# Scaled eviction of the dK, dV accumulator: from ScalarE to VectorE

## The chip, the cores and the metric

The kernel runs on one core of a Trainium2 chip. The metric is the device time of one execution in microseconds (us). The engines are TensorE (PE in the profile; PEld is its weight load), VectorE (DVE), ScalarE (ACT), GpSimd (POOL) and SyncE (SP, which here issues DMAs).

## The reference

The program computes a transformer block (adaptive layer norm, attention with 32 heads of 16 columns, layer norm, a squared-ReLU MLP) on 2048 tokens of width 512, and the gradients of its inputs by jax.vjp. What matters here is attention:

```
qkv = (x @ wqkv).reshape(B, S, 3, H, Dh).transpose(2, 0, 3, 1, 4)
q, k, v = (qkv[0], qkv[1], qkv[2])
scale = Dh ** (-0.5)
scores = jnp.einsum('bhqd,bhkd->bhqk', q, k) * scale
p = _softmax(scores, axis=-1)
o = jnp.einsum('bhqk,bhkd->bhqd', p, v)
```

Its backward pass needs, per head, P again from q and k, dP = dO V^T, dS = P * (dP - rowsum(dO * O)), dV = P^T dO, dK = scale * dS^T Q and dQ = scale * dS K. (The kernel folds the row sum and the softmax's denominator into operands, so that dS is one multiplication of the PSUM result dP by the exponentials.)

## The kernel before

The program runs in phases: projections and the forward attention, with the MLP and its gradients worked in between (0 to about 1170 us of the profile), the backward attention loop (`attn_bwd`, about 1170 to 2420 us), and the remaining weight gradients and the gradient of x. The change touches the loop alone.

The loop goes over 8 groups `g` of four heads, two pairs `jp` in each, four **chunks** `c` of 512 keys, and 16 blocks `ib` of 128 queries, in groups of `G = 4` blocks; `i` is the block's place in its group. So there are 8 x 2 x 4 = 64 chunks of 16 blocks. One block, called a step below, does for each of two heads `a`:

- TensorE: scores into `st` (L1568, three PSUM buffers), and, one block behind, dP into `dp` (L1494, three PSUM buffers);
- ScalarE: the exponential of `st` into `pu` (L1571);
- VectorE: dS = `dp` * `pu` into the bf16 tile `ds` (L1498).

In every second group of four blocks (`off`, L1500) the multiplication of the first block's second head goes another way: ScalarE copies `dp` to SBUF (L1506) and GpSimd multiplies (L1507). In the other groups TensorE transposes a part of `ds` itself (`turn_ds`, L1527) and ScalarE copies it to `dsT` (L1528). The rest of `ds` is transposed by a DMA that SyncE issues (L1515).

Some blocks later, every second block calls `kv_two`, which calls `kv` (L1442) for two blocks: eight matmuls add dS^T Q and P^T dO into `acckv`, one PSUM tile of 128x512 (L1448). The blocks between call `dq` (L1470), which adds dS K into `accq`. `acckv` has a single buffer. After the 16th block of a chunk, `kv` moves it to the bf16 tile `kvT`, scaled per partition by `kvs` (L1451): `kvs` holds 0.25 on the first 64 partitions (dK) and 1 on the others (dV). The matmuls run four or five blocks behind, so this eviction comes in the fourth step (`i` = 3) of the first group of the next chunk, behind that step's scores, exponentials and dS. The next chunk's first accumulator matmul must wait for it. When the four chunks of a pair of heads are done, `turn` transposes `kvT` back on TensorE (L1459) and ScalarE copies it out (L1463); `accq` is scaled by the constant 0.25 on VectorE (L1477).

Order: in this phase the instructions of TensorE, SyncE and GpSimd run in the order in which the program writes them. Those of VectorE and ScalarE are ordered by the scheduler that builds the program. Each engine runs its own instructions in order.

Of the kernel before, what the change touches and what calls it, by code (L numbers as in the profile page):

```python
# [11 lines left out]
ACT = mybir.ActivationFunctionType  # L12
ALU = mybir.AluOpType
# [92 lines left out]
class K:  # L106
# [1315 lines left out]
    def attn_bwd(self):  # L1422
# [7 lines left out]
        tc, nc = self.tc, self.nc  # L1430
# [5 lines left out]
        acckv = accp.tile([P, 512], F32, name="acckv")  # L1436
        nc.vector.memset(acckv[:], 0.0)
        accq = accp.tile([P, ST, 2, DH], F32, name="accq")
        masked, kvs = self.masked, self.kvs
        pend, pendq = [], []  # L1440

        def kv(u):  # L1442
            (T, g, jp, c, ib, kvT, pu, ds) = u
            for j, (n, src) in enumerate((("Q", ds), ("dO", pu))):
                for a in range(2):
                    r = 64 * j + 32 * a
                    col = (2 * jp + a) * DH
                    nc.tensor.matmul(acckv[r:r + DH, :], lhsT=T[n][:, ib, col:col + DH], rhs=src[:, a, :],  # L1448
                                     start=(ib == 0), stop=(ib == ST - 1))
            if ib == ST - 1:  # L1450
                nc.scalar.activation(kvT[:, 512 * c:512 * (c + 1)], acckv[:], ACT.Copy, scale=kvs[:])  # L1451

        def turn(g, jp, kvT, s0):

# [24 lines left out]
        def kv_two(n=2):  # L1479
            for u in pend[2 - n:2]:  # L1480
                kv(u)
            (T, g, jp, c, ib, kvT, pu, ds) = pend[1]
            del pend[:2]
            if c % 2 and ib == ST - 1 and (g, jp) == (NQ - 1, 1):
                turnq.append((g, jp, kvT, 4 * (c - 1)))
            elif c == SC - 1 and ib == ST - 1:
                turnq.extend((g, jp, kvT, s0) for s0 in (0, ST // 2))
# [45 lines left out]
        for g in range(NQ):  # L1533
            for jp in range(2):
# [13 lines left out]
                kvT = kvp.tile([P, S], BF16, name="kvT")  # L1548
# [36 lines left out]
        with tc.manual_schedule(engines=ALL):  # L1585
            for t in (2, 0):
                for p in self.wq_pieces(t):
                    nc.gpsimd.dma_start(*p)
            for a in range(2):
                dP(last, a)  # L1590
            dS(last)
            while len(pend) > 2:
                kv_two()
            kv(pend[0])
            for _ in range(G):
                dq(pendq.pop(0), [0, 1])
            kv_two(1)
            k0, v0, k1 = [dpp.tile([P, 512], F32, name="dp") for _ in range(3)]
            self.dw_mm(k0, 1, 0, 0, ST // 2)
            turn(*turnq.pop(0))  # L1600
            for _ in range(G):
                dq(pendq.pop(0), [0, 1])
            self.dw_mm(v0, 2, 0, 0, ST // 2)
            self.dw_mm(k0, 1, 0, ST // 2, ST)
            self.col_sum(1)
            self.dw_mm(v0, 2, 0, ST // 2, ST)
            self.col_sum(2)
            self.cs_bc(1)
            while pendq:
                dq(pendq.pop(0), [0, 1])  # L1610
            self.cs_bc(2)
            self.dw_mm(k1, 1, 1, 0, ST)
# [312 lines left out]
```

## Time and profile before

| | |
|---|---|
| median of 3 runs | 2545.73 us (2542.11 to 2547.05) |
| the profiled execution | 2545.66 us, of which the span is 2543.9 |
| busy over the span | PE 2453.8, ACT 2299.9, DVE 1700.3, POOL 707.1 us |
| DVE L1498, dS | 1920 of 681 ns, busy 1169.9 us |
| ACT L1571, exponentials | 2048 of 626 ns, busy 1075.8 us |
| ACT L1451, the eviction | 64 of 687 to 717 ns, first start 1194.4, last 2418.0 us |
| PE L1448, accumulator matmuls | 4096 |

A group's row gives the line, the engine, the operation, what is written and read, the number, then busy time and mean ns of one, and the idle time of the engine just before it with what ended it. In a view in order of time the columns are start, length, engine, line and operation, with neighbours of one kind merged into one row (x13); the idle time before the first of them stands in brackets. PE's ends are modelled, so its matmuls overlap in the rows and its busy share reads high. Two instructions of one engine can overlap by their pipelining: busy time of a row is then less than number times mean.

### The profile page before, as it was taken

To read this page: it belongs to the slowest core of one execution; us is meant where nothing else is said; L and a number is where in the kernel's file an instruction comes from. 1 tells how busy PE (TensorE), PEld (TensorE's weight loads), DVE (VectorE), ACT (ScalarE), POOL (GpSimd) and SP (SyncE) were. 2 spreads that over 40 slices of the span, in tenths; PEclk is the share of its full clock that TensorE was granted. 3 is DMA by queue.
4 is the path that set the end of the run, shared out by engine and by line. 5 is a ranking of instruction groups with operands and counts; after the bars stand their busy time and mean duration, and the time that the engine had idled before them with its cause. 6 is when DMAs were issued, how large, how long until landed. Compare 5 with 4: busy or idle time off the path is not lost.

```text
span 2543.9 us, 76653 instructions
## 1 busy us (share of the span) xinstructions
PE 2453.8 (96%) x30727; PEld 1201.3 (47%) x30727; DVE 1700.3 (67%) x3523; ACT 2299.9 (90%) x3757; POOL 707.1 (28%) x1265
## 2 busy tenths in 40 slices
PE   8999899999999999999999999999999999999998
PEld 4555555555555554663444444444444444443443
DVE  6222223423332343677999999999999999999957
ACT  7999999999999997436999999999999999999935
POOL 2454521220231031354222222222222222222223
PEclk9999999999999999999999999999999999999999
DMA  4588652440351053898999999999999999999996
GB/s 165 117 179 197 169 106 80 103 116 23 107 135 49 22 162 102 165 208 197 221 219 216 217 217 218 218 216 213 216 219 217 219 218 214 217 220 233 231 211 175
DMA packets 1258571, 442.07 MB, mean 174 GB/s; under 512 B 1203540, under 2 KB 1227222, under 8 KB 1258214
## 3 DMA queue, kind: packets, MB, share of 16 engines
q1 hardware_dynamic: 1219078, 336.03, 68.1%
q0 software_dynamic: 37056, 100.11, 13.2%
q8 instruction: 240, 3.93, 0.6%
q10 hardware_dynamic: 2080, 1.05, 0.1%
q14 instruction: 117, 0.96, 0.1%
HBM read 73.73 MB, written 62.40 MB: 54 GB/s over the span
## 4 chain that ended last, share of the span: by engine, by line
PE 58%; ACT 26%; DMA 8%; issue 5%; DVE 2%; POOL 1%; SPq 0%; DVEq 0%; ACTq 0%; POOLq 0%
ACT pu L391 18%; PE st L1568 15%; PE st L388 8%; PE acckv L1448 8%; PE accq L1470 7%; DMA dsT<-ds 7%; ACT pu L1571 6%; PE accbank L322 3%; PE dp L1494 2%; PE dps L1047 2%; PE pps L1234 2%; PE dp L1618 1%; PE pps L631 1%; PE dps L992 1%; PE st L1713 1%
## 5 line engine op out<-in xcount | busy, mean ns | idle before, releaser
L1498 DVE TENSOR_TENSOR ds<-dp,pu 128x512 bf16<-128x512 f32 x1920 | 1169.9, 681 | 67.9 <-PE dp L1494 46.6
L1571 ACT ACTIVATE pu<-st 128x512 bf16<-128x512 f32 x2048 | 1075.8, 626 | 49.1 <-PE st L1568 21.3
L391 ACT ACTIVATE pu<-st 128x1024 bf16<-128x1024 f32 x992 | 912.0, 1077 | 3.1 <-PE st L388 2.9
L388 PE MATMUL st<-QTm,KTq 128*128 128x512 bf16 x1984 | 587.7, 377 | 19.5 <-ACT pu L391 6.0
L322 PEld LDWEIGHTS <-pu 128*128 128x128 bf16 x8192 | 347.6, 96 | 235.7 <-issue 2.3
L322 PE MATMUL accbank<-Vaug,pu 128*128 128x17 bf16 x8192 | 357.7, 171 | 1.2 <-ACT Vaug L522 0.9
L1470 PEld LDWEIGHTS <-dsT 128*128 128x128 bf16 x8192 | 240.1, 96 | 229.4 <-issue 199.8
L1494 PE MATMUL dp<-m,q 64*128 64x512 bf16 x1024 | 344.4, 382 | 1.6 <-DVE g2w L1053 0.7
L1494 PE MATMUL dp<-m,dOTg 64*128 64x512 bf16 x1024 | 344.2, 382 | 0.1
L1568 PE MATMUL st<-m,QTg 64*128 64x512 bf16 x1024 | 322.1, 381 | 12.2 <-ACT pu L1571 7.5
L1568 PE MATMUL st<-m,q 64*128 64x512 bf16 x1024 | 321.6, 382 | 11.3 <-ACT pu L1571 6.7
L388 PEld LDWEIGHTS <-KTq 128*128 128x128 bf16 x1984 | 187.9, 96 | 176.1 <-issue 124.5
L1507 POOL TENSOR_TENSOR ds<-junk,pu 128x512 bf16<-128x512 f32 x64 | 74.1, 1157 | 412.6 <-ACT junk L1506 412.6
L302 POOL DMA_DIRECT2D QTm<-QTq_d x124 | 63.1, 511 | 341.0 <-PE st L388 319.5
L1448 PE MATMUL acckv<-ds,Qg 128*16 128x512 bf16 x1024 | 154.5, 382 | 0.0
L1448 PE MATMUL acckv<-pu,dOg 128*16 128x512 bf16 x1024 | 154.4, 382 | 0.0
L1448 PE MATMUL acckv<-pu,q 128*16 128x512 bf16 x1024 | 154.0, 381 | 0.0
L1448 PE MATMUL acckv<-ds,q 128*16 128x512 bf16 x1024 | 154.0, 381 | 0.0
L1470 PE MATMUL accq<-Kg,dsT 128*128 128x16 bf16 x4096 | 143.7, 170 | 10.3 <-DMA dsT<-ds 9.9
L1507 POOL TENSOR_TENSOR ds<-csq,pu 128x512 bf16<-128x512 f32 x64 | 73.9, 1154 | 281.5 <-ACT csq L1506 281.5
L1470 PE MATMUL accq<-q,dsT 128*128 128x16 bf16 x4096 | 144.6, 170 | 3.8 <-DMA dsT<-ds 3.6
L329 DVE RECIPROCAL rl<-accbank 128x4 f32<-128x4 f32 x128 | 22.9, 179 | 159.6 <-PE accbank L322 159.4
(383 smaller groups left out, 2980.3 us busy)
## 6 DMA issues: line engine op xcount, KB each, us to landing
KTq<-KTq_d POOLq DMA_DIRECT2D x24, 512.0 KB, 4.0
duT_d<-auT POOLq DMA_DIRECT2D x3, 1792.0 KB, 7.9
aT_d<-rT POOLq DMA_DIRECT2D x3, 1792.0 KB, 11.3
KTq_d<-KTq SPq DMA_DIRECT2D x32, 128.0 KB, 1.8
QTq_d<-ev_fm SPq DMA_DIRECT2D x32, 128.0 KB, 3.9
VTq_d<-vT POOLq DMA_DIRECT2D x4, 1024.0 KB, 6.5
dsT<-ds SPq DMA_TRANSPOSE x256, 7.2
dx<-dx_d SPq DMA_DIRECT2D x16, 256.0 KB, 5.6
```

The source lines that it names most:

```text
L302: nc.gpsimd.dma_start(QTm[j][32 * j:32 * j + 32, :], self.QTq_d[g, 32 * j:32 * j + 32, 512 * qc:512 * (qc + 1)])
L322: nc.tensor.matmul(acc[:, a, sub, :], lhsT=pu[:, a, sub * P:(sub + 1) * P], rhs=Vaug[:, kb, h, :], start=(kb == 0 and a == 0 and sub == 0) ...
L388: nc.tensor.matmul(stt[:, a, :], lhsT=KT[:, kb * P:(kb + 1) * P], rhs=QTm[2 * jp + a][:], start=True, stop=True)
L391: nc.scalar.activation(pu[:], stt[:], ACT.Exp, scale=self.scale)
L1047: nc.tensor.matmul(pt[:], lhsT=a[st], rhs=g_tm[:, st, :], start=(st == 0), stop=(st == ST - 1))
L1448: nc.tensor.matmul(acckv[r:r + DH, :], lhsT=T[n][:, ib, col:col + DH], rhs=src[:, a, :], start=(ib == 0), stop=(ib == ST - 1))
L1470: nc.tensor.matmul(accq[:, ib, a, :], lhsT=dsT[:, (i * 2 + a) * 4 + sub, :], rhs=T["K"][:, 4 * c + sub, col:col + DH], start=(c == 0 and i ...
L1494: nc.tensor.matmul(dp[:], lhsT=T["dOT"][rd, ib * P:(ib + 1) * P], rhs=masked["VT"][2 * jp + a][rd, 512 * c:512 * (c + 1)], start=True, sto ...
L1498: nc.vector.tensor_tensor(dsg[:, i, a], dp[:], pu[:, a, :], ALU.mult)
L1507: nc.gpsimd.tensor_tensor(dsg[:, i, 1], f[:], pu[:, 1, :], ALU.mult)
L1568: nc.tensor.matmul(stt[:], lhsT=T["QT"][rs, q], rhs=masked["KT"][2 * jp + a][rs, c0:c0 + 512], start=True, stop=True)
L1571: nc.scalar.activation(pu[:, a, :], stt[:], ACT.Exp, scale=self.scale)
```

## The change

The eviction is computed by VectorE's `tensor_scalar` with the per-partition scalar `kvs`, in place of ScalarE's activation with the same scalar as its scale. Input, output, formats and place in the program are as before.

```diff
             if ib == ST - 1:
-                nc.scalar.activation(kvT[:, 512 * c:512 * (c + 1)], acckv[:], ACT.Copy, scale=kvs[:])
+                nc.vector.tensor_scalar(kvT[:, 512 * c:512 * (c + 1)], acckv[:], kvs[:], None, ALU.mult)
```

## The prediction

> **What bounds the kernel now.** I began with the share of busy time by stage, because the line that changes runs only in the backward attention loop (1172 to 2418 us). Two of its 64 chunks, and 200 us of it, look like this (columns: length, then busy time and instructions of PE, its weight loads, DVE, ACT, POOL, then clock, DMA share, GB/s):
>
> ```profile
> core 0: us, PE busy (x) PEld busy (x) DVE busy (x) ACT busy (x) POOL busy (x), PEclk, DMA share, GB/s
> 1600.00:1800.00 200.00, 195.12 (x2756) 82.28 (x2752) 188.82 (x311) 194.72 (x391) 46.21 (x90) 1.00 1.13 217
> ```
>
> ACT is busy 97%, DVE 94%, PE 98% (with modelled ends). By these shares VectorE has the room. A share says nothing about where in a chunk it lies, so I read the order of time next: first VectorE alone, then ScalarE, then TensorE, around the eviction of one chunk.
>
> ```profile
> 1811.57 7.85 DVE L1498 TENSOR_TENSOR ds<-dp,pu 128x512 bf16<-128x512 f32 x13
> 1819.91 3.74 DVE L1498 TENSOR_TENSOR ds<-dp,pu 128x512 bf16<-128x512 f32 x6 [0.49 <-PE dp L1494]
> 1823.90 5.47 DVE L1498 TENSOR_TENSOR ds<-dp,pu 128x512 bf16<-128x512 f32 x9 [0.25 <-PE dp L1494]
> ```
>
> Thirteen multiplications of 0.68 us take 7.85: one starts every (7.85 - 0.68) / 12 = 0.598 us, which is also the median of all 1920. VectorE has no hole in the stretch in which the eviction runs; its hole (0.49 in this view) comes behind it, where GpSimd takes one multiplication.
>
> ```profile
> 1816.31 1.09 ACT L1571 ACTIVATE pu<-st 128x512 bf16<-128x512 f32 x2
> 1817.28 0.70 ACT L1451 ACTIVATE kvT<-acckv,kvs 128x512 bf16<-128x512 f32 x1
> 1817.85 2.09 ACT L1571 ACTIVATE pu<-st 128x512 bf16<-128x512 f32 x4
> 1819.76 0.66 ACT L1506 COPY junk<-dp 128x512 f32<-128x512 f32 x1
> ```
>
> ```profile
> 1816.81 0.39 PE L1568 MATMUL st<-m,q 64*128 64x512 bf16 x1
> 1817.90 0.39 PE L1494 MATMUL dp<-m,q 64*128 64x512 bf16 x1
> 1818.52 0.37 PE L1568 MATMUL st<-m,q 64*128 64x512 bf16 x1 [0.23 <-ACT pu L1571]
> 1818.53 0.39 PE L1494 MATMUL dp<-m,q 64*128 64x512 bf16 x1
> 1818.84 0.39 PE L1448 MATMUL acckv<-ds,q 128*16 128x512 bf16 x2
> 1819.38 0.39 PE L1494 MATMUL dp<-m,q 64*128 64x512 bf16 x1
> ```
>
> Elsewhere a step's first exponential starts 0.42 to 0.47 us after its score matmul starts (medians at 9 of a chunk's 16 steps; the matmul's own 0.37 is in it), so there ScalarE has no queue. Behind the eviction it has one: the scores of 1816.81 are read only at 1817.85, and TensorE stands at 1818.52 for a score buffer.
>
> For VectorE I went by single records. There are three dP buffers, so a dP matmul needs the multiplication three before it to have ended. It starts 0.05 us after that end, held by VectorE, at 10 of the 32 places of a chunk (medians over 62 chunks), three in each group but the one behind the eviction: in three of four groups VectorE paces TensorE and not the reverse. The commonest period of a chunk is 18.89 us. VectorE's 30 multiplications take 30 x 0.598 = 17.94 of it; 0.95 is idle, nearly all in the two holes: 0.57 (median) in the group behind the eviction, 0.31 in the other group that gives one to GpSimd. The two holes have the same program around them, except that the first has the eviction ahead of it on ScalarE. I read their difference, 0.26, as ScalarE's lag.
>
> **The change part by part.** *Removed:* 64 ScalarE instructions of 0.70 us. The exponential behind one starts 0.57 after it, so ScalarE is relieved by 64 x 0.57 = 36 us. That shortens the loop only where ScalarE's lag reaches VectorE: 0.26 per chunk.
>
> *Added:* 64 VectorE instructions. Their shape, 128x512 f32 in PSUM to bf16, has two near rows:
>
> ```profile
> L1212 DVE TENSOR_SCALAR rT<-pps,bias 128x512 bf16<-128x512 f32 x42 | 31.5, 751 | 105.4 <-PE pps L1209 105.4
> L1477 DVE TENSOR_SCALAR dq_t<-accq 128x512 bf16<-128x512 f32 x16 | 10.9, 681 | 18.0 <-PE accq L1470 18.0
> ```
>
> L1477 scales by a constant: 0.681, and the next instruction starts 0.598 after it. L1212 takes its scalar per partition from SBUF, as the new instruction does (kvs): 0.751, and 0.667 at its shortest to the next start. Scalar_tensor_tensor shows the same split, 691 with constants and 750 with a per-partition operand, so the 0.07 belongs to the operand and not to L1212's second operation. I take 0.67; bounds 0.60 and 0.75 (no overlap with the next).
>
> [...]
>
> *Where it lands.* In program order the eviction follows the two multiplications of step 4 of a chunk's first group. In the stretch shown these are the 9th and 10th of the thirteen (starts 1816.35 and 1816.95), so it starts at 1817.55. Its last accumulator matmuls start at 1816.49 and last 0.38, so it waits for nothing (0.68 to spare). Queued behind it are the 11th to 13th; TensorE waits for them through the dP buffers. Then:
> - The 11th starts at 1818.22 instead of 1817.55 and ends at 1818.90.
> - The second dP matmul of step 6, which needs that buffer, starts at 1818.95 instead of 1818.53: +0.42. Its loss of 0.67 is cut by 0.25 because the old start stood behind ScalarE (1818.52 above).
> - The accumulator matmuls follow 0.31 later, the next dP 0.54 after those, at 1819.80; VectorE starts 0.53 after it, at 1820.33 instead of 1819.91. It was free at 1820.01: the hole is now 0.32, as in the other group.
> - From there TensorE catches up, since ScalarE no longer holds it at step 8, but VectorE runs without a break and takes back only the 0.04 to 0.05 of idle time there.
>
> So each chunk grows by 0.37 to 0.42; I take 0.39. The sum by slots agrees: 17.94 + 0.67 + 2 x 0.31 + 0.07 = 19.30 against 18.89, +0.41. The next chunk's first accumulator matmul must now wait for VectorE rather than ScalarE; it stands behind the dP matmul that already waits for the 11th multiplication, so that wait costs nothing more. No DMA is issued by the moved step. The turns of kvT come three steps behind and move with TensorE; in the 16 chunks that have them TensorE's transposes follow the same dP matmul, so they shift by the same amount. Of the 64 evictions the last lies in the tail, where both engines wait for TensorE (2.2 us): 0.05 there at most.
>
> *Against it:* TensorE's waits for the transposed dS, which lands 7.2 us after its issue (median), sum to 23.6 us on its weight loads. Transfers issued ahead of the eviction and read behind it gain its delay. VectorE's idle time at those two places is 3.4 and 1.8 us over the loop (means over medians); I let 4 us of it go.
>
> Sum: 63 x 0.39 = 24.6, less 4, about **+20 us**. The profiled execution took 2545.66 us, of which 2543.9 are its span and 1.8 lie around it; the median of the runs is 2545.73, so it serves as the base: 2545.7 + 20 = **2566 us**. By the bounds of the price (0.60 and 0.75, gaining 0.32 and 0.47 per chunk, all 5 or none absorbed): 2561 and 2575.
>
> **The rivals.** *The holes take it in (2546 us).* VectorE's order is not written by hand in this phase (only TensorE's, SyncE's and GpSimd's are), so the eviction could be placed behind the 13th multiplication, in the hole. Then 0.57 of its 0.67 is covered and the rest, 0.10 x 63 = 6 us, goes against the ScalarE lag and the waits for dS. For it: 0.95 idle per chunk exceeds 0.67. Against it: it is ready 0.68 before the 11th, so nothing calls for a later place.
>
> *ScalarE is the pace (2532 us).* Its 97% and the chain of waits, where exponentials have more of the loop than VectorE, speak for it. If its load causes both holes, a chunk falls to 17.94 + 0.67 + 0.07 = 18.68, -0.21 x 63 = -13 us. It decides if TensorE is still found waiting for exponentials where VectorE is free. Against it: exponentials mostly start as soon as their scores are there, and TensorE waits for a score buffer only 14.0 us in the whole loop.
>
> *Nothing comes back from ScalarE (2588 us).* If the hole of 0.57 has another cause, such as the copy for GpSimd (0.66 here, 0.59 in the other group), the whole price stays: 63 x 0.67 = 42 us.
>
> **How the numbers follow.** Chances: forecast 0.66, holes take it in 0.12, ScalarE the pace 0.09, nothing back 0.13. A change within 0.2% (5 us, 2541 to 2551) can't be told from none here. The forecast's own range is 2556 to 2576; to hold 8 in 10 it reaches down into the second case and up to the last, 2549 to 2588. Faster 0.09, same 0.12, slower 0.66 + 0.13 = 0.79.
>
> **What would show it.** VectorE's row for L1451: 64 of about 0.75 us, no idle time before them; 0.68 or 0.70 would mean the per-partition operand is free. The commonest chunk about 19.3 us. The waits of L1568 for exponentials (14.0 us) nearly gone, ScalarE about 94% busy and VectorE 97%. The hole behind the eviction at 0.3. I am wrong if the eviction stands in that hole, if chunks without a turn stay at 18.89, or if the hole stays at 0.57.

## The result and the profile after

| | before | changed |
|---|---|---|
| median of 6 runs each, side by side | 2541.42 us | 2563.23 us (2559.0 to 2566.08) |
| ratio | | 1.0083, 95% interval 1.0067 to 1.0100 |
| span of the profiled execution | 2543.9 us | 2563.8 us |
| commonest chunk / mean chunk of the loop | 18.89 / 19.47 us | 19.23 / 19.78 us |

The kernel is 22 us slower (17 to 25 by the interval). The spans differ by 19.9; the mean chunk grew by 0.306, and 63 x 0.306 = 19.3: in these two executions the loss lies in the loop.

Two rows of the groups of the changed kernel, and its 200 us of the loop by stage (columns as before):

```profile
L1498 DVE TENSOR_TENSOR ds<-dp,pu 128x512 bf16<-128x512 f32 x1920 | 1171.4, 680 | 49.2 <-PE dp L1494 45.2 <-ACT pu L1571 1.6 <-ACT junk L1506 0.2
L1451 DVE TENSOR_SCALAR kvT<-acckv,kvs 128x512 bf16<-128x512 f32 x64 | 47.3, 739 | 0.7 <-PE acckv L1448 0.7
```

```profile
core 0: us, PE busy (x) PEld busy (x) DVE busy (x) ACT busy (x) POOL busy (x), PEclk, DMA share, GB/s
1600.00:1800.00 200.00, 195.10 (x2738) 78.05 (x2731) 193.46 (x320) 190.50 (x377) 46.90 (x92) 1.00 1.10 214
```

The eviction takes 0.739 us and waits for nothing but 0.7 us once, in the tail. ScalarE fell from 97% to 95% busy, VectorE rose from 94% to 97%. The same chunk as before, first VectorE, then ScalarE, then TensorE, in order of time:

```profile
1823.81 6.06 DVE L1498 TENSOR_TENSOR ds<-dp,pu 128x512 bf16<-128x512 f32 x10
1829.79 0.74 DVE L1451 TENSOR_SCALAR kvT<-acckv,kvs 128x512 bf16<-128x512 f32 x1
1830.45 1.87 DVE L1498 TENSOR_TENSOR ds<-dp,pu 128x512 bf16<-128x512 f32 x3
1832.55 9.06 DVE L1498 TENSOR_TENSOR ds<-dp,pu 128x512 bf16<-128x512 f32 x15 [0.23 <-PE dp L1494]
```

```profile
1828.56 3.07 ACT L1571 ACTIVATE pu<-st 128x512 bf16<-128x512 f32 x6
1831.59 0.58 ACT L1506 COPY junk<-dp 128x512 f32<-128x512 f32 x1
```

```profile
1830.35 0.38 PE L1568 MATMUL st<-m,q 64*128 64x512 bf16 x1
1831.18 0.37 PE L1494 MATMUL dp<-m,q 64*128 64x512 bf16 x1 [0.46 <-DVE ds L1498]
1831.48 0.39 PE L1448 MATMUL acckv<-ds,q 128*16 128x512 bf16 x2
1832.03 0.39 PE L1494 MATMUL dp<-m,q 64*128 64x512 bf16 x1
```

VectorE evicts without a hole on either side (1829.79, next start 1830.45: a slot of 0.66). The multiplication behind it ends at 1831.13 (1830.45 + 0.68), and TensorE's second dP matmul of step 6 starts at 1831.18. Before, the score matmul beside it stood for ScalarE; now it goes at 1830.35 and the dP matmul stands for VectorE. Over the loop (1200 to 2400 us; waits: us in total, times, longest) the one wait has taken the other's place, and that for the transposed dS has not shrunk:

```profile
PE st L1568 <- ACT pu L1571: 13.7, 55, 0.3
PEld L1470 <- DMA dsT<-ds: 23.6, 43, 1.8
```

```profile
PEld L1470 <- DMA dsT<-ds: 26.3, 41, 1.9
PE dp L1494 <- DVE ds L1498: 24.9, 57, 0.5
```

The first two lines are of before, the others of the changed kernel, which has no wait of `st` for `pu` among its waits. The hole behind the eviction (extra time between two multiplications, median over 62 chunks) fell from 0.57 to 0.31.

### The profile page after: what moved, and what is told of

The parts are those of the page before. It is cut to its first block, busy times and chain, and to the rows that moved or that the text cites. A ratio compares the mean times of both kernels' runs of the same rounds, so it can differ in the third digit from the quotient of the medians.

```text
span 2563.8 us, 76589 instructions
## 1 busy us (share of the span) xinstructions
PE 2469.2 (96%) x30727; PEld 1182.4 (46%) x30727; DVE 1737.7 (68%) x3587; ACT 2285.6 (89%) x3693; POOL 706.8 (28%) x1265
## 4 chain that ended last, share of the span: by engine, by line
PE 63%; ACT 19%; DMA 8%; DVE 4%; issue 4%; POOL 1%; DVEq 0%; SPq 0%; ACTq 0%; POOLq 0%
ACT pu L391 18%; PE st L1568 17%; PE acckv L1448 9%; PE st L388 8%; PE accq L1470 8%; DMA dsT<-ds 7%; PE dp L1494 4%; PE accbank L322 3%; DVE ds L1498 2%; PE dps L1047 2%; PE pps L1234 2%; PE dp L1618 1%; PE pps L631 1%; DVE kvT L1451 1%; PE st L1713 1%
## 5 line engine op out<-in xcount | busy, mean ns | idle before, releaser
L1568 PE MATMUL st<-m,q 64*128 64x512 bf16 x1024 | 312.4, 381 | 1.0
L1568 PE MATMUL st<-m,QTg 64*128 64x512 bf16 x1024 | 312.4, 381 | 0.9
```

The source lines that it names most:

```text
L1568: nc.tensor.matmul(stt[:], lhsT=T["QT"][rs, q], rhs=masked["KT"][2 * jp + a][rs, c0:c0 + 512], start=True, stop=True)
```

## The experiments

Chunk times and holes below come from the single records of each trace, as medians over chunks 2 to 63. A chunk is counted "with turns" when `turn` runs in it, which is every fourth. The times were taken in three sets, each beside its own runs of before (medians 2547.74, 2543.88 and 2546.70 us): the first four kernels below in one, the next three and the one in the hole in another, the rest in the last. Means and waits come from the one profiled execution of each kernel. In the code, `...` marks lines left out.

**No eviction at all.** `kvT` is one tile, zeroed once:

```diff
-                nc.scalar.activation(kvT[:, 512 * c:512 * (c + 1)], acckv[:], ACT.Copy, scale=kvs[:])
+                pass
...
-                kvT = kvp.tile([P, S], BF16, name="kvT")
+                kvT = kvT0
```

> Leaves out: the eviction of the accumulator altogether (dK and dV come from a zeroed tile). All else is the kernel before. Theory (VectorE paces; ScalarE's eviction costs only the lag that reaches VectorE behind it): the hole behind the old place of the eviction shrinks from 0.57 to 0.31 us, the commonest chunk from 18.89 to 18.63, the time by 63 x 0.26 = 16 us. Rival 1 (the longer hole has another cause, such as the copy for GpSimd): no change. Rival 2 (ScalarE is the pace): 0.57 per chunk, 36 us faster.

Measured: 2532.59 us, ratio 0.9943 (0.9925 to 0.9960), that is 10 to 19 us faster; commonest chunk 18.58; hole 0.31. The hole of 0.57 was ScalarE's lag: the copy for GpSimd is still there and the hole is not. What ScalarE's eviction cost the loop was 0.31 per chunk, and relieving ScalarE of its 0.57 was worth no more than that. The time is as forecast. The mean chunk fell only from 19.47 to 19.32 in the profiled execution, which was the slowest of the five (2543.45 us, 11 over their median); in it TensorE's waits for the transposed dS grew:

```profile
PEld L1470 <- DMA dsT<-ds: 43.9, 62, 3.7
```

**The eviction split between the engines by partitions.**

```diff
-                nc.scalar.activation(kvT[:, 512 * c:512 * (c + 1)], acckv[:], ACT.Copy, scale=kvs[:])
+                sl = slice(512 * c, 512 * (c + 1))
+                nc.scalar.activation(kvT[0:64, sl], acckv[0:64], ACT.Copy, scale=kvs[0:64])
+                nc.vector.tensor_scalar(kvT[64:P, sl], acckv[64:P], kvs[64:P], None, ALU.mult)
```

> The eviction split by partitions: ScalarE moves 0 to 63, VectorE 64 to 127, so each engine pays a whole instruction (its length goes by the 512 columns). Theory (TensorE's second dP matmul of step 6 waits for the later of the two engines, so the two delays do not add): as the changed kernel, commonest chunk 19.23, about 21 us slower than before (within 4). Rival (the price and ScalarE's lag add up): 63 x 0.66 = 42 us slower than before, chunk 19.55.

Measured: 2578.30 us, ratio 1.0124 (1.0105 to 1.0143): 31 us slower, chunk 19.47, between the two. It doesn't decide. Each part did cost a whole instruction or nearly: 0.757 us on VectorE and 0.677 on ScalarE for 64x512, against 0.739 and 0.702 for 128x512. VectorE's part was placed one multiplication later than in the changed kernel, and its slot is longer (first VectorE's rows, then ScalarE's):

```profile
1501.41 3.07 DVE L1498 TENSOR_TENSOR ds<-dp,pu 128x512 bf16<-128x512 f32 x5
1504.52 0.76 DVE L1451 TENSOR_SCALAR kvT<-acckv,kvs 64x512 bf16<-64x512 f32 x1
1505.31 1.29 DVE L1498 TENSOR_TENSOR ds<-dp,pu 128x512 bf16<-128x512 f32 x2
```

```profile
1503.54 0.68 ACT L1451 ACTIVATE kvT<-acckv,kvs 64x512 bf16<-64x512 f32 x1
1504.11 2.04 ACT L1571 ACTIVATE pu<-st 128x512 bf16<-128x512 f32 x4
```

ScalarE's part had ended 0.30 us before VectorE's started (1503.54 + 0.68 = 1504.22). But VectorE's starts 0.04 after the multiplication ahead of it has ended (1504.48), and the next multiplication 0.03 after its own end (1505.28), where in the changed kernel it overlaps both by 0.08. So its slot, counted as the extra time between the two multiplications around it, is 0.90 instead of 0.66. Why the overlap is lost was not tested.

**The hole moved ahead of the eviction, the eviction on ScalarE.** In the kernel before:

```diff
-            return (c * SC + ib // G) % 2 == 1
+            return (c * SC + ib // G) % 2 == 0
```

> The kernel before (eviction on ScalarE) with the parity of off() turned over: GpSimd takes its multiplication in groups 1 and 3 of a chunk counted from 1, the group of the eviction among them, and not in the one behind it. Theory: ScalarE's lag behind the eviction now meets a group in which VectorE has a queue of dP in hand, so it no longer opens a hole: chunk 18.63, 16 us faster than before. Rival (the lag costs its 0.26 wherever it falls): no change. Rival (moving the copy for GpSimd beside the eviction makes ScalarE later still): slower by some us.

Measured: 2544.74 us, ratio 0.9990 (0.9970 to 1.0011): no difference that can be told. The commonest chunk did fall to 18.58, both holes at 0.31, a little below the 18.63 expected; the time did not follow. The chunks with turns grew from 20.54 to 20.85, and the waits for the transposed dS doubled (in an execution of 2554.12 us, the slowest of ten):

```profile
PEld L1470 <- DMA dsT<-ds: 52.1, 81, 2.5
```

**The same turn of parity with the eviction on VectorE.**

> The changed kernel (eviction on VectorE) with the parity of off() turned over as in the run before. Theory: VectorE's work is 30 x 0.598 + 0.66 and two holes of 0.31 per chunk wherever the holes lie, so chunk 19.23 and the time of the changed kernel, about 21 us slower than before (within 4). Rival (a hole in the same group lends its idle time to the eviction): 0.31 per chunk back, about 2 us slower than before.

Measured: 2578.77 us, ratio 1.0126 (1.0106 to 1.0145): 31 us slower. The chunk is 19.24 and both holes 0.31, as the theory has it: a hole earlier in the same group lends the eviction nothing. The time is some 10 us over what was expected: the chunks with turns are longer again (21.16 against 20.86, some 5 us in all), and the waits for dS are about twice those of the changed kernel (51.7 against 26.3 us).

**The changed kernel again**, as the base for the next two and for the one in the hole.

> The changed kernel again, beside the next runs on one chip: about 21 us slower than before.

Measured: 2570.99 us, ratio 1.0104 (1.0087 to 1.0120); chunk 19.23. That is 27 us over before (22 to 31), where the runs side by side above had 22 (17 to 25): with the same commonest chunk, the cost in time came out 5 us apart.

**A constant in place of the per-partition operand.**

```diff
-                nc.vector.tensor_scalar(kvT[:, 512 * c:512 * (c + 1)], acckv[:], kvs[:], None, ALU.mult)
+                nc.vector.tensor_scalar(kvT[:, 512 * c:512 * (c + 1)], acckv[:], 1.0, None, ALU.mult)
...
-                nc.scalar.copy(d, v[:, t, :, :, 0:DH])
+                nc.scalar.activation(d, v[:, t, :, :, 0:DH], ACT.Copy, scale=1.0 if t else self.scale)
```

> The changed kernel with the constant 1.0 as VectorE's scalar; the factor 0.25 of dK is applied by ScalarE's copies out of the turned tile, which are instructions of the kernel already. Theory (the per-partition operand makes the eviction's slot 0.66 instead of 0.60): eviction 0.68 long, chunk 19.16 to 19.17, 4 us faster than the changed kernel. Rival (the slot is set by the shape alone): no difference.

Measured: 2566.35 us, ratio to before 1.0090 (1.0072 to 1.0107), 4.6 us below the base by the medians. The intervals overlap, so the time does not settle it. The trace settles the slot: the row of the eviction has 678 ns where the changed kernel has 739, its slot is 0.60 and the commonest chunk 19.17. The mean chunk did not fall with it (19.81 in the profiled execution of either), so a gain in time is not shown.

```profile
L1451 DVE TENSOR_SCALAR kvT<-acckv 128x512 bf16<-128x512 f32 x64 | 43.4, 678 | 0.7 <-PE acckv L1448 0.7
```

**The eviction twice on VectorE** (the changed line written twice).

> The changed kernel with the eviction done twice on VectorE, same input and output. Theory (nothing is left to regain from ScalarE and VectorE has no usable room): the second one costs its whole slot, 0.66 x 63 = 42 us more than the changed kernel, chunk 19.89. Rival (VectorE's two holes of 0.31 take in a part): about 20 us more.

Measured: 2596.41 us, ratio 1.0214 (1.0194 to 1.0235): 25 us over the base, chunk 19.57, which is 0.34 more and not 0.66. The rival was right here. The second eviction was placed one multiplication further on, and the hole behind it is gone. So VectorE does have room for 0.3 us, at one place: behind the multiplication whose end TensorE waits for. The next two runs follow from that.

**One multiplication later.** The eviction is put off until the next step's first multiplication is issued, with VectorE's order written by hand:

```diff
-                nc.vector.tensor_scalar(kvT[:, 512 * c:512 * (c + 1)], acckv[:], kvs[:], None, ALU.mult)
+                late.append((kvT, c))
...
-                                nc.scalar.activation(pu[:, a, :], stt[:], ACT.Exp, scale=self.scale)
+                                nc.scalar.activation(pu[:, a, :], stt[:], ACT.Exp, scale=self.scale); late and i == 0 and a == 0 and evict(*late.pop())
```

> The changed kernel with VectorE's eviction one multiplication later (behind the first of step 5 instead of ahead of it; VectorE's order written by hand in this phase, all else as in the changed kernel). Theory (what the eviction costs is what it adds ahead of the multiplication that the second dP matmul of step 6 waits for; behind that one it runs into the hole): TensorE's next accumulator matmul waits for it 0.1 to 0.4 us, the hole behind it nearly closes, chunk 18.97 to 19.05, some 5 us slower than before and 15 faster than the changed kernel. Rival (VectorE pays its 0.66 wherever it stands): as the changed kernel, 21 us slower than before.

Measured: 2558.79 us, ratio 1.0063 (1.0042 to 1.0085). The commonest chunk is 18.97, and the chunks with turns 20.56 (before: 20.54), as the theory has it. VectorE now runs through the place of the hole (four multiplications on end behind the eviction):

```profile
1842.83 4.28 DVE L1498 TENSOR_TENSOR ds<-dp,pu 128x512 bf16<-128x512 f32 x7 [0.45 <-PE dp L1494]
1847.02 0.74 DVE L1440 TENSOR_SCALAR kvT<-acckv,kvs 128x512 bf16<-128x512 f32 x1
1847.68 2.50 DVE L1498 TENSOR_TENSOR ds<-dp,pu 128x512 bf16<-128x512 f32 x4
```

(L1440 is where this kernel's `evict` stands.) But the time is 11 to 22 us over before, not 5. The changed kernel was 22 (17 to 25) and 27 us (22 to 31) over, so a gain in time over it is not clear beside the first of these. The waits for dS rose to 37.8 us, and the mean of the chunks without turns is 19.47 against 19.10. The chunk answers the question that was put; why these waits grew is open. No run has VectorE's order written by hand with the eviction at its old place, so what that alone does to the waits is not known either.

**Two multiplications later**, with `a == 1` in place of `a == 0` in that line.

> The same, but two multiplications later. Theory: TensorE's accumulator matmuls of step 6 now stand 0.7 us for the eviction to end, and the next dP with them: chunk about 19.55, 42 us slower than before. Rival (the later, the nearer the hole): at or below the kernel one later.

Measured: 2580.78 us, ratio 1.0137 (1.0118 to 1.0157): 30 to 40 us slower, less than the 42 expected; chunk 19.53. The waits for dS are shorter (14.2 us, before 23.6). TensorE's accumulator matmuls now stand for the eviction:

```profile
PE acckv L1448 <- DVE kvT L1440: 51.9, 59, 0.9
```

**In the hole itself**, with `i == 1 and a == 0`.

> The changed kernel with the eviction moved behind the first multiplication of step 6, that is into VectorE's hole (VectorE's order written by hand in this phase, otherwise the same order on all engines). Rival to the theory (the hole is room for it): about the time of before. Theory (the single accumulator makes TensorE wait: its next accumulator matmuls, which come in that very step, stand 1.5 us later behind the eviction, and the next dP with them, so the hole grows to 1.2): chunk about 20.1, some 57 us slower than the changed kernel (40 to 70).

Measured: 2645.50 us, ratio 1.0409 (1.0387 to 1.0432): 75 us over the base, more than the 40 to 70 expected. The commonest chunk is 20.13, as expected; others are 1 us longer, in an execution whose granted clock was 0.94 to 0.98 through the loop (1.00 in the changed kernel), and the two were not separated. The wait is the one that the theory named:

```profile
PE acckv L1448 <- DVE kvT L1440: 83.1, 56, 1.8
```

**Half of the dS transposes, in the kernel before.**

```diff
-                nc.sync.dma_start_transpose(dsT[:, n:, :], dsg[:].rearrange("p i a k -> p (i a k)")[:, n * P:])
+                nc.sync.dma_start_transpose(dsT[:, n:4 * G, :], dsg[:].rearrange("p i a k -> p (i a k)")[:, n * P:4 * G * P])
...
-                    nc.tensor.matmul(accq[:, ib, a, :], lhsT=dsT[:, (i * 2 + a) * 4 + sub, :],
+                    nc.tensor.matmul(accq[:, ib, a, :], lhsT=dsT[:, (i % 2 * 2 + a) * 4 + sub, :],
```

> Leaves out: the DMA's transposition of the second half of every group's dS (dQ takes the first half twice, with as many matmuls). All else is the kernel before. Theory (TensorE's waits for transposed dS cost up to 0.2 us per chunk over the commonest period, 63 x 0.2 = 13 us): 5 to 13 us faster than before, commonest chunk still 18.89. Rival (the transposes are hidden): no change.

Measured: 2536.94 us, ratio 0.9975 (0.9956 to 0.9993), that is 2 to 11 us faster; commonest chunk 18.90, mean of the chunks without turns 18.94 (before: 19.10), in an execution of 2546.97 us, 10 over the median. No wait for dsT is left among TensorE's.

**The same with the parity turned over and the eviction on ScalarE.**

> The same part left out of the kernel with off() turned over and the eviction on ScalarE. Theory (that kernel's chunk fell to 18.58 as expected, but waits for transposed dS, twice as long as before, took the gain): with those gone it is 63 x 0.3 = 19 us faster than the run before this one (12 to 20). Rival (the gain was lost in the chunks with turns, or elsewhere on the engines): no faster than the run before this one.

Measured: 2522.77 us, ratio to before 0.9916 (0.9893 to 0.9939), 14 us below the run before this one. Here the chunks without turns are 18.61 in the mean, 18.57 at the median, but those with turns stay at 20.84, against 20.54 in the run before. So with all transposes in place the turned parity loses its gain in two ways. Most of it goes to the waits for the transposes: with half of them left out 14 us stay, with all of them 3. Some 5 us (16 x 0.3) go to the chunks with turns, which the transposes do not explain. This run's DMA share (the last number but one) is half of before's 1.13:

```profile
1600.00:1800.00 200.00, 197.22 (x2803) 83.31 (x2800) 191.30 (x316) 195.86 (x398) 49.30 (x95) 1.00 0.55 111
```

No version that keeps the whole computation beat the kernel before by more than its interval.

## Why the prediction was right

*The bound.* VectorE paces the commonest chunk at three groups of four, though its share of busy time was the lowest of the three engines (94% against 97% and 98%, 1600 to 1800 us). Shown by the run without an eviction and by the constant operand: 0.57 us taken off ScalarE gave 0.31 per chunk, and 0.06 taken off VectorE's slot gave 0.06. One reading of the prediction was off by one: of its ten places where a dP matmul starts 0.05 us after the instruction that frees its buffer, nine follow a multiplication of VectorE, three in each of three groups. The tenth, in the group behind the eviction, follows ScalarE's copy for GpSimd (in the chunk shown the copy ends at 1820.42 and the matmul starts at 1820.46).

*The price.* 0.67 was taken from the row with a per-partition operand; the slot is 0.66, the length 0.739. The split by operand kind held: 0.678 and 0.60 with a constant.

*The place.* No wait ahead of it, the second dP matmul of step 6 held by the 11th multiplication, the hole at 0.32: measured none, 0.46 us of waiting there (1831.18), and 0.31. From the multiplication ahead of the eviction to the first behind the hole the changed kernel takes 0.40 more (2.96 to 3.36 us); the walk had 0.42.

*The sum.* The commonest chunk grew by 0.34, a little less than the walk's 0.37 to 0.42 and the 0.41 of the slots: the few hundredths of idle time behind the hole, which the slots carried on as 0.07, are all but gone (30 x 0.598 + 0.66 + 2 x 0.31 = 19.22 of 19.23). They were ScalarE's lag too, for they are gone without an eviction as well, so the lag was worth 0.31 per chunk and not 0.26. The chunks with turns grew by 0.32, as good as the others, as was said.

*Against it.* This term was wrong: 4 us were to be taken in by waits for the transposed dS. These went from 23.6 to 26.3 us, and nothing was taken in. The two misses nearly cancel, 63 x 0.34 = 21 against 24.6 - 4, so that +20 came this close to the measured +22 is in part luck.

*The rivals.* "Nothing comes back" fell with the hole at 0.31 after the change and without any eviction. "ScalarE is the pace" fell with the run without an eviction: at most 19 us for 36 us of relief. "The holes take it in" was half right in a way that I had not seen. Put in the hole, the eviction costs far more (75 us over the base), since the accumulator has one buffer and TensorE waits for it (83.1 us). But one multiplication later than the scheduler put it, 0.26 of its slot of 0.66 is hidden (chunk 18.97 against 19.23; without an eviction 18.58).

*Not foreseen.* The transposes of dS are a second bound close behind VectorE: two kernels with a commonest chunk of 18.58 or 18.97 (the turned parity on ScalarE, one later) gained less than their chunk says. That the transposes take most of the gain is shown for the turned parity, by the two runs with half of them; for one later it is read from its waits. Why turning the parity doubles those waits, with the same transposes, and why it makes the chunks with turns 0.3 longer, is open.

## What to carry to other kernels

Before work is moved to an engine with a lower busy share, see whether the other engines stand for it at the place where the work will land: here a TensorE matmul started 0.05 us after a multiplication of VectorE at 9 of 32 places. When one instruction moves between two engines that are both near the pace, count the slot on the new one less only the part of the old one's lag that reached the pace: here 0.66 less 0.31, against 0.34 measured. And the eviction of a single accumulator had a narrow place here: early enough for the next accumulation, and behind the instruction that the others wait for (chunk 18.97 there, 19.23 one multiplication earlier, 19.53 one later).

## What the runs showed of the hardware

- A `tensor_scalar` with a per-partition operand took VectorE 0.739 us, with a constant 0.678, at the same 128x512 from PSUM; the slots are 0.66 and 0.60.
- Half the partitions saved nothing on VectorE and little on ScalarE: 64x512 took VectorE 0.757 us and ScalarE 0.677, against 0.739 and 0.702 for 128x512. VectorE's, on the partitions from 64 up, also lost the overlap of 0.08 us with the instruction on either side.
- With the second half of the DMA transposes left out, TensorE's waits for them on its weight loads went from 23.6 us to none (1200 to 2400 us). With the parity turned over as well there was none either, at a DMA share of 0.55 against 1.13 before (1600 to 1800 us).
